# Weight preparation reordered: ScalarE's rounding one row later, three staging buffers, and the weights' stores and loads on another queue in the gated block

## The chip, the cores and the metric

The kernel runs on one core of a Trainium2 chip. The metric is the device time of one execution in microseconds (us). The parts of the core are TensorE (PE in the profile, its weight loads PEld), VectorE (DVE), ScalarE (ACT), GpSimd (POOL) and SyncE (SP). Each of them takes its instructions in the order in which they were issued. SyncE and GpSimd here mostly start transfers (DMAs); a transfer that has to wait for something holds up all that stands behind it in the same queue.

## The reference

Two blocks run one after the other. The first is attention with a hash: for each of 4 x 8 heads of 768 positions and 64 features, six sign bits of `q @ proj` and `k @ proj` give a bucket, and a query attends only to keys of its own bucket.

```python
scores = scale * np.matmul(q, k.transpose(0, 1, 3, 2))
scores = np.where(mask, scores, -1000000000.0)
attn = np.exp(scores - max); attn = attn / (sum + 1e-09)
out = np.matmul(attn, v)
```

The second is a gated block on the 3072 x 512 matrix that the heads make side by side:

```python
g = x @ w_gate                    # 512 x 1536
silu = g * (1.0 / (1.0 + np.exp(-g)))
val = x @ w_val
return (silu * val @ w_out)       # 1536 x 512
```

The three weight matrices come as 64-bit floats.

## The kernel before

**Attention part.** Heads are worked on in 16 pairs; the first four pairs are the first batch. A pair is two halves of 384 queries, and a half is what is called a row here: six units (`score(u)`, one per 128 keys). A unit is four score matmuls, two with `qT`/`kT` and two with the bits `qb`/`kb`, and two exponentials on ScalarE (L431). After the six units of a row come the 24 products with v (`attend`, L442). VectorE adds the exponentials of a row (`add`, L459 and L463), ScalarE copies the result out (L452), and a pair later the sums are made (`total`, L474, its copy L477), inverted (L483), spread by transfers over SyncE's queue, and the result is normalized (`norm`, L498). For the first batch the normalized result is split in three parts for the second block (`split`, L201, L204, L208); for the other batches it goes to memory (`kept_x`). Queries and keys are transposed on TensorE with copies on ScalarE (L342, L345) for the first pairs (`n <= NP`, 4) and on VectorE for the rest (L396).

**Weight preparation.** The weights are cut into 36 pieces of 128 x 512 doubles. Each piece is loaded into a word buffer (L116), and turned into three 32-bit parts in a staging buffer, and the staging buffer is stored (`ram`, L154) to be read again once per batch. This runs beside the attention, and what is left of it beside the first batch of the gated block. For piece i:

- `scale(i)`: two ScalarE passes (L123, L124), from the word buffer into the staging buffer and back into the word buffer.
- VectorE: shift (L141), sign (L143), addition (L146).
- ScalarE: the rounding (L147), which reads what L146 wrote.
- VectorE: the subtraction (L150) and the remainder (L152); then the store (L154).

`prepare()` is a generator with one VectorE step between two yields; `prepare_on(n)` runs n steps. Each row issues five steps (pairs 1 to 3) or four (the others) at its end, behind all else of the row, 134 of 180 in all; each atom of the gated block issues one. `scale_ahead()` is called between a row's scores and its products with v, and once after these; it issues the scaling of the next piece when at most two pieces are open. There are four word buffers and two staging buffers. All loads and stores of pieces but the first two loads stand on GpSimd's queue. The order of all this is the order of the calls; nothing plans it anew.

**Gated block.** For each of 4 batches, 12 blocks of columns (`U`: four groups of matmuls, tiles `a` and `n`, for gate and value; two atoms each) and 4 output steps (`D`: six chunks, tile `o`). All matmuls are at L584. PSUM holds four double banks in turn. The three parts of a weight piece are read into a ring of seven buffers (`bring`, L190), on GpSimd's queue, which also carries the pieces still in preparation. Three blocks before a batch ends, the next batch's `kept_x` is loaded on SyncE's queue (L700) into word buffers (`spare`) and split, one step per atom. The last pair's result and its spread sums sit in word buffers too; their inversion and normalization are issued at the 6th and the 14th atom of the block.

Of the kernel before, what the change touches and what calls it, by code (L numbers as in the profile page):

```python
# [19 lines left out]
def kernel(  # L20
# [20 lines left out]
    nc = tc.nc  # L41
    PSUM = bass.MemoryType.PSUM
    B, H, S, D = q.shape
    NBITS = proj.shape[1]
    P = 128
# [4 lines left out]
    NP = H // 2  # L50
# [4 lines left out]
    PIECE = 512  # L55
# [7 lines left out]
    STEP = 4096.0  # L63
    TOWARD = 1 - 2.0**-13

    konst = ctx.enter_context(tc.tile_pool(name="konst", bufs=1))
    wordp = ctx.enter_context(tc.tile_pool(name="wordp", bufs=4))
    stagep = ctx.enter_context(tc.tile_pool(name="stagep", bufs=2))
    small = ctx.enter_context(tc.tile_pool(name="small", bufs=2))
    even_x = ctx.enter_context(tc.tile_pool(name="even_x", bufs=1))  # L70
    ringp = ctx.enter_context(tc.tile_pool(name="ringp", bufs=7))
    dram = ctx.enter_context(tc.tile_pool(name="dram", bufs=1, space=bass.MemoryType.DRAM))
    ctx.enter_context(tc.manual_schedule())
# [3 lines left out]
    def r32(t):  # L77
        return t.bitcast(FP32R)
# [16 lines left out]
    n = 0  # L95
# [8 lines left out]
    NPIECE = len(pieces)  # L104
    ram = [dram.tile([P, 3, PIECE], FP32R, tag=f"ram{i}", name="ram") for i in range(NPIECE)]
    words = {}
    staged = {}
    progress = {"scaled": 0, "kept": 0}

    def load_words(count, queue=nc.gpsimd):  # L110
        for i in range(len(words), min(count, NPIECE)):
            words[i] = t = wordp.tile([P, PIECE, 2], I32, tag="words", name="words")
            to = t.rearrange("p f w -> p (f w)")
            if len(pieces[i].shape) == 3:
                to = to.rearrange("p (j c) -> p j c", j=NJ)
            queue.dma_start(to, pieces[i])  # L116

    def scale(i):
        t = words[i]
        staged[i] = st = stagep.tile([P, 3, PIECE], FP32, tag="stage", name="stage")  # L120
        top = t.rearrange("p f w -> p (f w)").bitcast(U16)
        top = top.rearrange("p (f w) -> p f w", w=4)[:, :, 1]
        nc.scalar.activation(st[:, 1], t[:, :, 1].bitcast(FP32), AF.Copy, scale=2.0**-112)  # L123
        nc.scalar.activation(t[:, :, 0], top, AF.Copy, scale=2.0**-13 * (1 + 2.0**-17))  # L124
        progress["scaled"] = i + 1

    def scale_ahead():
        i = progress["scaled"]
        if i < NPIECE and i < progress["kept"] + 2 and i in words:
            scale(i)  # L130

    def prepare():
        for i in range(NPIECE):
            load_words(i + 1)
            if i not in staged:
                scale(i)
            t, st = words[i], staged[i]
            lo, hi = t[:, :, 0], t[:, :, 1]
            w = st[:, 1]
            wi = w.bitcast(I32)  # L140
            nc.vector.tensor_single_scalar(wi, wi, 3, op=ALU.logical_shift_left)  # L141
            yield True
            nc.vector.scalar_tensor_tensor(out=wi, in0=hi, scalar=-(1 << 31), in1=wi,  # L143
                                           op0=ALU.bitwise_and, op1=ALU.bitwise_or)
            yield True
            nc.vector.tensor_tensor(wi, wi, lo, op=ALU.add)  # L146
            nc.scalar.activation(r32(st[:, 0]), w, AF.Copy, scale=TOWARD)  # L147
            load_words(i + 4)
            yield True
            nc.vector.tensor_tensor(r32(w), w, st[:, 0], op=ALU.subtract)  # L150
            yield True
            nc.vector.scalar_tensor_tensor(out=r32(st[:, 2]), in0=w, scalar=-STEP, in1=st[:, 0],  # L152
                                           op0=ALU.mult, op1=ALU.add)
            nc.gpsimd.dma_start(ram[i].bitcast(FP32), st)  # L154
            progress["kept"] = i + 1
            yield True

    preparing = prepare()

    def prepare_on(n):  # L160
        for _ in range(n):
            next(preparing, None)
# [33 lines left out]
    def split(x, b, pr, pool):  # L196
        xparts[b, pr] = t = pool.tile([P, 3, S], FP32R, tag=f"x{pr}", name="xparts")
        h, l, d = (t[:, i] for i in range(3))

        def high():  # L200
            nc.scalar.activation(h, x, AF.Copy, scale=TOWARD / STEP)  # L201

        def low():
            nc.vector.scalar_tensor_tensor(out=l, in0=h.bitcast(FP32), scalar=-STEP, in1=x,  # L204
                                           op0=ALU.mult, op1=ALU.add)

        def diff():
            nc.vector.tensor_tensor(d, h.bitcast(FP32), l.bitcast(FP32), op=ALU.subtract)  # L208

        return [high, low, diff]  # L210
# [3 lines left out]
    def attention(scope):  # L214
# [80 lines left out]
        for h in range(2):  # L295
# [6 lines left out]
                                op=ALU.mult)  # L302
# [18 lines left out]
        for i in range(RING):  # L321
            t = fixed.tile([P, 2, AW], FP32, tag=f"A{i}", name="A")
# [5 lines left out]
        load_words(2, nc.sync)  # L328
        for name, queue in (("q", nc.sync), ("k", nc.gpsimd), ("v", nc.sync)):
            fetch(1, name, queue)  # L330
        load_words(4)

        T = {}
        bits = {}
# [74 lines left out]
        acc = {}  # L409
        av = {}  # L410
        xT = {}
        mean = {}
        waiting = []

# [19 lines left out]
        def attend(u):  # L434
            n, half, c = units[u]
            a = weights(u)
            if c == 0:
                av[n] = av_ps.tile([P, 512], FP32, tag="av", name="av")
            ps = av[n]
            width = AW if half == 0 else HQ  # L440
            for h in range(2):
                nc.tensor.matmul(ps[h * D : (h + 1) * D, 0:width], raws["v", n][:, h, c, :],  # L442
                                 a[:, h, 0:width], start=c == 0, stop=c == NCH - 1)
            if c == NCH - 1:
                if half == 0:
                    if n == len(pairs) - 1:
                        xT[n] = spare()
                    else:
                        xT[n] = xp.tile([P, S], FP32, tag="xT", name="xT")
                    mean[n] = small.tile([P, 1], FP32, tag="e", name="e")  # L450
                    nc.scalar.activation(mean[n], ps[:, HQ : HQ + 1], AF.Copy, scale=EPS)
                nc.scalar.copy(xT[n][:, half * HQ : (half + 1) * HQ], ps[:, 0:HQ])  # L452
# [29 lines left out]
        def invert(n, few):  # L482
            nc.vector.reciprocal(few, few)  # L483
            s = sums[n % 2]
            nc.sync.dma_start(s, few)
            if n == len(pairs) - 1:
                t = spare().rearrange("p (x q) -> p x q", x=2)
            else:
                t = att.tile([P, 2, HQ], FP32, tag="r", name="r")
            flat = s.rearrange("p e -> (p e)").rearrange("(h x t) -> h (x t)", h=2, t=HQ)  # L490
            for h in range(2):
                nc.sync.dma_start(t[h * D : (h + 1) * D].rearrange("p x t -> p (x t)"),
                                  flat[h : h + 1].to_broadcast([D, 2 * HQ]))
            return lambda: norm(n, t)
# [13 lines left out]
        rest = []  # L508
# [48 lines left out]

    left = []

    def spare():  # L560
        t = wordp.tile([P, PIECE, 2], I32, tag="words", name="words")
        return t.rearrange("p f w -> p (f w)")[:, 0:S].bitcast(FP32)

    with ExitStack() as scope:
        attention(scope)

    def gated_block(scope):
        xs = [even_x, scope.enter_context(tc.tile_pool(name="odd_x", bufs=1))]  # L570
        hidp = scope.enter_context(tc.tile_pool(name="hidp", bufs=4))
        gatep = scope.enter_context(tc.tile_pool(name="gatep", bufs=2))
        outp = scope.enter_context(tc.tile_pool(name="outp", bufs=1))
# [41 lines left out]
        def atoms_of(kind, n):  # L615
# [33 lines left out]
            else:  # L649
# [35 lines left out]
                for c in range(NCH):  # L685
# [2 lines left out]
                        end(c)  # L688
                    yield chunk

        tails = []
        splits = []
        count = [0]
        for kind, n in order:
            if kind == "U":
                b, f = divmod(n, NF)
                if f == NF - NQ and b + 1 < B:
                    for pr in range(NP):
                        x = spare()
                        nc.sync.dma_start(x, kept_x[b + 1, pr])  # L700
                        splits += split(x, b + 1, pr, xs[(b + 1) % 2])
            if kind == "D" and n == B * NF // NQ - 1:
                finish(tails)
            for atom in atoms_of(kind, n):
                tail = atom()
                finish(tails)
                if tail:
                    tails.append(tail)
                if splits:
                    splits.pop(0)()  # L710
                count[0] += 1
                if left and count[0] in (6, 14):
                    left.append(left.pop(0)())
                    left[:] = [f for f in left if f]
                prepare_on(1)

    with ExitStack() as scope:
        gated_block(scope)
# [32 lines left out]
```

## Time and profile before

| | |
|---|---|
| median of 14 runs | 990.16 us (987.4 to 992.84) |
| the profiled execution | 992.84 us, its span 991.0 us |
| busy: TensorE, VectorE, ScalarE | 952.0, 674.8, 471.8 us |
| mean TensorE clock granted | 0.986 |
| first matmul of the gated block | at 385.47 us |

In a timeline row stand start and duration in us, the engine, the line of the kernel, the operation, the tiles as out<-in, the shapes, how many instructions were merged, and in brackets the idle time before it with what ended it. In a table of waits stand the total in us, how often, and the longest. In a table of stretches the numbers after the stretch are its length, the busy time of each engine with its count of instructions, the TensorE clock granted, the share of time the DMA engines were busy, and GB/s. In a row of grouped instructions the count is followed by the busy time, the mean duration of one in ns, and the engine's idle time before them with what ended it.

### The profile page before, as it was taken

Reading aid. Unit: us, or ns where it says so; the run is one execution under the profiler, and the core shown is the slowest. Engines: PE = TensorE matmul, PEld = TensorE weight load, DVE = VectorE, ACT = ScalarE, POOL = GpSimd, SP = SyncE. Lnnn points to the kernel's source line nnn. Section 1 sums busy time; section 2 is a strip of 40 time slices with the busy share of each in tenths; the row PEclk is TensorE's granted clock in tenths of the full one; section 3 lists DMA queues with packets and bytes.
Section 4 is the critical chain, followed back from the end, with each engine's and each line's share of the span. In section 5 each row is a group of like instructions: output and inputs, shape, how many; then the busy total and the mean of one; then the engine's idle time right before and its main releaser. Section 6 shows DMA issues by size and latency. Waiting matters only on the chain.

```text
span 991.0 us, 14470 instructions
## 1 busy us (share of the span) xinstructions
PE 952.0 (96%) x5413; PEld 726.8 (73%) x5413; DVE 674.8 (68%) x868; ACT 471.8 (48%) x882; POOL 125.1 (13%) x248
## 2 busy tenths in 40 slices
PE   8988899989899899999999999999999999999998
PEld 3444444444444346989999999999999999999996
DVE  4667678778878586868886546586546586546556
ACT  6867766877677485444322332322232322232221
POOL 3110010100101011131210110110110110110100
PEclk9989999999999899999999999999999999999999
DMA  6554566766878667499955854655854655654641
GB/s 181 175 154 133 160 173 139 212 181 188 202 170 217 198 242 251 165 353 374 344 201 187 321 191 157 224 190 191 319 189 161 223 186 193 259 186 165 223 160 64
DMA packets 134262, 203.22 MB, mean 205 GB/s; under 512 B 92912, under 2 KB 98512, under 8 KB 134192
## 3 DMA queue, kind: packets, MB, share of 16 engines
q0 software_dynamic: 31008, 159.79, 45.1%
q1 hardware_dynamic: 102384, 42.30, 17.3%
q8 instruction: 43, 0.70, 0.3%
q10 hardware_dynamic: 800, 0.20, 0.1%
q14 instruction: 27, 0.22, 0.1%
HBM read 162.01 MB, written 39.42 MB: 203 GB/s over the span
## 4 chain that ended last, share of the span: by engine, by line
PE 58%; DVE 1%; issue 1%; DMA 0%; ACT 0%; POOL 0%; POOLq 0%; DVEq 0%; ACTq 0%
PE a L584 27%; PE o L584 18%; PE n L584 13%; DVE o L676 0%; DVE o L673 0%; DMA ram<-stage 0%; ACT stage L123 0%; DVE words L498 0%; DVE hid L640 0%; DVE g L632 0%; DVE stage L143 0%; ACT words L124 0%; POOL words L116 0%; ACT o L671 0%; DVE stage L141 0%
## 5 line engine op out<-in xcount | busy, mean ns | idle before, releaser
L584 PE MATMUL a<-xparts,ring 128*128 128x384 f32 x1536 | 283.5, 335 | 1.9 <-ACT row L477 1.9
L584 PEld LDWEIGHTS a<-xparts,ring 128*128 128x128 f32 x1536 | 269.3, 188 | 3.8 <-ACT row L477 2.6
L584 PE MATMUL o<-ring,hid 128*128 128x512 f32 x864 | 199.4, 390 | 2.1 <-DVE o L676 2.1
L428 PE MATMUL sc<-qT,kT 64*128 64x384 f32 x768 | 176.4, 523 | 22.6 <-ACT A L431 22.6
L584 PEld LDWEIGHTS o<-ring,hid 128*128 128x128 f32 x864 | 161.8, 188 | 35.6 <-DVE o L676 2.5
L431 ACT ACTIVATE A<-sc 128x384 f32<-128x384 f32 x384 | 156.5, 503 | 9.1 <-PE sc L428 8.6
L584 PE MATMUL n<-xparts,ring 128*128 128x384 f32 x768 | 148.9, 335 | 0.0
L428 PEld LDWEIGHTS sc<-qT,kT 64*128 64x128 f32 x768 | 79.5, 193 | 93.7 <-issue 48.2
L463 DVE TENSOR_TENSOR acc<-acc,A 128x768 f32<-128x768 f32 x128 | 122.7, 958 | 25.0 <-ACT A L431 14.0
L584 PEld LDWEIGHTS n<-xparts,ring 128*128 128x128 f32 x768 | 135.0, 188 | 0.0
L442 PE MATMUL av<-A,vraw 128*64 128x386 f32 (+1 forms) x768 | 131.6, 491 | 0.0
L190 POOL DMA_DIRECT2D ring<-ram x144 | 76.2, 531 | 427.4 <-PE n L584 269.6
L632 DVE TENSOR_TENSOR v<-v,n 128x768 f32<-128x768 f32 x48 | 45.8, 954 | 104.6 <-PE n L584 103.1
L442 PEld LDWEIGHTS av<-A,vraw 128*64 128x64 f32 x768 | 52.4, 137 | 73.0 <-issue 62.0
L626 ACT ACTIVATE g<-a 128x768 f32<-128x768 f32 x48 | 38.9, 810 | 127.1 <-PE a L584 122.6
L637 ACT ACTIVATE hid<-v 128x768 fp32r<-128x768 f32 x48 | 40.7, 847 | 117.5 <-DVE v L636 117.5
L428 PE MATMUL sc<-qb,kb 64*128 64x384 bf16 x384 | 79.5, 335 | 5.2 <-DMA qb<-qb 4.6
L634 ACT ACTIVATE g<-g 128x768 f32<-128x768 f32 x48 | 40.6, 847 | 89.6 <-DVE g L632 89.6
L676 DVE TENSOR_TENSOR o<-o 128x512 f32<-128x512 f32 x96 | 66.0, 687 | 22.1 <-ACT o L671 19.7
L632 DVE TENSOR_TENSOR g<-g,n 128x768 f32<-128x768 f32 x48 | 45.6, 950 | 35.0 <-PE n L584 34.9
L154 POOL DMA_DIRECT2D ram<-stage x36 | 19.5, 542 | 369.1 <-issue 142.9
L640 DVE SCALAR_TENSOR_TENSOR hid<-hid,v 128x768 fp32r<-128x768 f32 x48 | 45.9, 956 | 26.2 <-ACT hid L637 26.2
(77 smaller groups left out, 712.4 us busy)
## 6 DMA issues: line engine op xcount, KB each, us to landing
ring<-ram POOLq DMA_DIRECT2D x144, 768.0 KB, 5.6
ram<-stage POOLq DMA_DIRECT2D x36, 768.0 KB, 5.0
vraw<-in_v_dram SPq DMA_DIRECT2D x16, 384.0 KB
words<-in_moe_w_out_dram POOLq DMA_DIRECT2D x12, 512.0 KB, 7.4
out_dram<-o SPq DMA_DIRECT2D x24, 256.0 KB
r<-sums SPq DMA_DIRECT2D x30, 192.0 KB
words<-in_moe_w_gate_dram POOLq DMA_DIRECT2D x11, 512.0 KB, 6.8
words<-in_moe_w_val_dram POOLq DMA_DIRECT2D x11, 512.0 KB, 7.5
```

What stands on the lines that cost most here:

```text
L190: nc.gpsimd.dma_start(t.bitcast(FP32), ram[at].bitcast(FP32))
L428: nc.tensor.matmul(sc[h], x["k", n][rows, ks], x["q", n][rows, qs], start=start, stop=not start)
L431: nc.scalar.activation(weights(u)[:, h, 0:HQ], sc[h], AF.Exp, scale=SCALE * (OFF / 2 if n <= NP else 1.0))
L442: nc.tensor.matmul(ps[h * D : (h + 1) * D, 0:width], raws["v", n][:, h, c, :], a[:, h, 0:width], start=c == 0, stop=c == NCH - 1)
L463: nc.vector.tensor_tensor(acc[n, half], acc[n, half], a[:, :, 0:HQ], op=ALU.add)
L584: nc.tensor.matmul(ps, w, x, start=start, stop=stop)
L626: nc.scalar.activation(two(z), ops[what][2], AF.Copy, scale=STEP + 1)
L632: nc.vector.tensor_tensor(two(z), two(z), n_, op=ALU.subtract)
L634: nc.scalar.activation(z, z, AF.Silu)
L637: nc.scalar.activation(h, val, AF.Copy, scale=TOWARD / STEP)
L640: nc.vector.scalar_tensor_tensor(out=l, in0=h.bitcast(FP32), scalar=-STEP, in1=val, op0=ALU.mult, op1=ALU.add)
L676: nc.vector.tensor_tensor(accs[c], accs[c], t[:, 1], op=ALU.subtract)
```

## The change

- Three word buffers instead of four, three staging buffers instead of two. Loads run up to piece i+2 instead of i+3. In the attention part scaling may run three pieces ahead of the stores (two in the gated block).
- The rounding of a piece is no longer issued with its addition. It goes on a list, `unrounded`, and the next call of `scale_ahead()` issues it before any scaling. The subtraction, the remainder and the store of piece i-1 come after the addition of piece i.
- In the gated block the preparation's loads and stores are on SyncE's queue, and `scale_ahead()` is called after each atom's step. Before the first reload of `kept_x` the preparation is run to its end.
- The last pair's result and its spread sums go into a buffer that later holds a part of a batch's x (`odd_x`), not into word buffers.

```diff
-    wordp = ctx.enter_context(tc.tile_pool(name="wordp", bufs=4))
-    stagep = ctx.enter_context(tc.tile_pool(name="stagep", bufs=2))
+    wordp = ctx.enter_context(tc.tile_pool(name="wordp", bufs=3))
+    stagep = ctx.enter_context(tc.tile_pool(name="stagep", bufs=3))
...
+    odd_x = {NP - 1: ctx.enter_context(tc.tile_pool(name="odd_x", bufs=1))}
...
-    progress = {"scaled": 0, "kept": 0}
+    progress = {"scaled": 0, "kept": 0, "ahead": 3}
+    queues = [nc.gpsimd]
...
+    unrounded = []
+
+    def round_up():
+        st = staged[unrounded.pop(0)]
+        nc.scalar.activation(r32(st[:, 0]), st[:, 1], AF.Copy, scale=TOWARD)
+
     def scale_ahead():
+        if unrounded:
+            round_up()
         i = progress["scaled"]
-        if i < NPIECE and i < progress["kept"] + 2 and i in words:
+        if i < NPIECE and i < progress["kept"] + progress["ahead"] and i in words:
             scale(i)

     def prepare():
-        for i in range(NPIECE):
...
+        for i in range(NPIECE + 1):
+            if i < NPIECE:
...
+                nc.vector.tensor_tensor(wi, wi, lo, op=ALU.add)
+                unrounded.append(i)
+                load_words(i + 3)
+                yield True
+            if i > 0:
+                while i - 1 in unrounded:
+                    round_up()
+                st = staged[i - 1]
+                w = st[:, 1]
+                nc.vector.tensor_tensor(r32(w), w, st[:, 0], op=ALU.subtract)
+                yield True
+                nc.vector.scalar_tensor_tensor(out=r32(st[:, 2]), in0=w, scalar=-STEP,
+                                               in1=st[:, 0], op0=ALU.mult, op1=ALU.add)
+                queues[0].dma_start(ram[i - 1].bitcast(FP32), st)
+                progress["kept"] = i
+                yield True
...
                     if n == len(pairs) - 1:
-                        xT[n] = spare()
+                        t = odd_x[NP - 1].tile([P, 3, S], FP32, tag=f"x{NP - 1}", name="lastx")
+                        xT[n], spread[n] = t[:, 0], t[:, 1]
...
-                t = spare().rearrange("p (x q) -> p x q", x=2)
+                t = spread[n].rearrange("p (x q) -> p x q", x=2)
...
+        queues[0] = nc.sync
+        progress["ahead"] = 2
...
                 if f == NF - NQ and b + 1 < B:
+                    while next(preparing, None):
+                        pass
                     for pr in range(NP):
...
                 prepare_on(1)
+                scale_ahead()
```

More of the change, by code (lines that the diff above doesn't have):

```diff
@@ L107, with load_words @@
     staged = {}
-    progress = {"scaled": 0, "kept": 0}
-    def load_words(count, queue=nc.gpsimd):
+    progress = {"scaled": 0, "kept": 0, "ahead": 3}
+    queues = [nc.gpsimd]
+    def load_words(count, queue=None):
+        queue = queue or queues[0]
         for i in range(len(words), min(count, NPIECE)):
@@ L125, in scale @@
         progress["scaled"] = i + 1
+    unrounded = []
+    def round_up():
+        st = staged[unrounded.pop(0)]
+        nc.scalar.activation(r32(st[:, 0]), st[:, 1], AF.Copy, scale=TOWARD)
     def scale_ahead():
+        if unrounded:
+            round_up()
         i = progress["scaled"]
-        if i < NPIECE and i < progress["kept"] + 2 and i in words:
+        if i < NPIECE and i < progress["kept"] + progress["ahead"] and i in words:
             scale(i)
     def prepare():
-        for i in range(NPIECE):
[L134 to L156, printed above, removed]
@@ new lines, in prepare @@
+        for i in range(NPIECE + 1):
+            if i < NPIECE:
+                load_words(i + 1)
+                if i not in staged:
+                    scale(i)
+                t, st = words[i], staged[i]
+                lo, hi = t[:, :, 0], t[:, :, 1]
+                wi = st[:, 1].bitcast(I32)
+                nc.vector.tensor_single_scalar(wi, wi, 3, op=ALU.logical_shift_left)
+                yield True
+                nc.vector.scalar_tensor_tensor(out=wi, in0=hi, scalar=-(1 << 31), in1=wi,
+                                               op0=ALU.bitwise_and, op1=ALU.bitwise_or)
+                yield True
[9 more added lines that the diff above has]
+                nc.vector.tensor_tensor(r32(w), w, st[:, 0], op=ALU.subtract)
+                yield True
+                nc.vector.scalar_tensor_tensor(out=r32(st[:, 2]), in0=w, scalar=-STEP,
+                                               in1=st[:, 0], op0=ALU.mult, op1=ALU.add)
+                queues[0].dma_start(ram[i - 1].bitcast(FP32), st)
+                progress["kept"] = i
+                yield True
@@ L330, in attention @@
             fetch(1, name, queue)
-        load_words(4)
+        load_words(3)
         T = {}
@@ L411, in attention @@
         xT = {}
+        spread = {}
         mean = {}
@@ L558 @@
     left = []
-    def spare():
-        t = wordp.tile([P, PIECE, 2], I32, tag="words", name="words")
-        return t.rearrange("p f w -> p (f w)")[:, 0:S].bitcast(FP32)
     with ExitStack() as scope:
@@ L569, in gated_block @@
     def gated_block(scope):
-        xs = [even_x, scope.enter_context(tc.tile_pool(name="odd_x", bufs=1))]
+        rest = scope.enter_context(tc.tile_pool(name="odd_x_rest", bufs=1))
+        xs = [dict.fromkeys(range(NP), even_x), {**dict.fromkeys(range(NP - 1), rest), **odd_x}]
         hidp = scope.enter_context(tc.tile_pool(name="hidp", bufs=4))
@@ L697, in gated_block @@
                 if f == NF - NQ and b + 1 < B:
+                    while next(preparing, None):
+                        pass
                     for pr in range(NP):
-                        x = spare()
+                        t = wordp.tile([P, PIECE, 2], I32, tag="words", name="words")
+                        x = t.rearrange("p f w -> p (f w)")[:, 0:S].bitcast(FP32)
                         nc.sync.dma_start(x, kept_x[b + 1, pr])
-                        splits += split(x, b + 1, pr, xs[(b + 1) % 2])
+                        splits += split(x, b + 1, pr, xs[(b + 1) % 2][pr])
             if kind == "D" and n == B * NF // NQ - 1:
```

## The prediction, made before the changed kernel ran

> **What bounds the kernel now.** I read the page first, then busy time by stretch, then who waits for whom on TensorE and ScalarE, then the timelines around the stalls.
>
> ```profile
> span 991.0 us, 14470 instructions
> PE 952.0 (96%) x5413; PEld 726.8 (73%) x5413; DVE 674.8 (68%) x868; ACT 471.8 (48%) x882; POOL 125.1 (13%) x248
> PEclk9989999999999899999999999999999999999999
> ```
>
> TensorE is busy for 96% of the span, so only its 39 us of idle time and the stretches at a lower clock can be won. The stretches below are cut at the row-sum matmuls (tile `sum`), one group per head pair: first pair 1 alone, then pairs 2 to 5, pairs 6 to 13, pair 14 alone, pair 15, and the gated block in two parts.
>
> ```profile
> core 0: us, PE busy (x) PEld busy (x) DVE busy (x) ACT busy (x) POOL busy (x), PEclk, DMA share, GB/s
> 33.17:54.90 21.73, 21.73 (x150) 10.12 (x149) 14.65 (x19) 19.44 (x43) 1.30 (x2) 1.00 0.63 188
> 54.90:161.12 106.22, 93.95 (x571) 45.26 (x569) 77.56 (x103) 75.39 (x168) 9.70 (x16) 0.92 0.57 157
> 161.12:344.70 183.58, 168.81 (x1090) 77.56 (x1088) 144.80 (x194) 126.88 (x293) 16.99 (x29) 0.98 0.73 188
> 344.70:365.38 20.68, 20.43 (x138) 8.89 (x136) 16.36 (x23) 17.08 (x40) 2.06 (x4) 1.00 0.73 254
> 365.38:385.47 20.09, 18.18 (x127) 8.04 (x125) 16.73 (x23) 14.72 (x35) 3.44 (x7) 1.00 0.66 234
> 435.33:991.00 555.67, 550.67 (x2922) 518.12 (x2921) 353.11 (x436) 172.51 (x225) 72.47 (x137) 1.00 0.60 217
> ```
>
> Two pairs run clean: pair 1 (which still transposes on TensorE) in 21.73, pair 14 in 20.68, both at full clock. Measured by these, pairs 2 to 5 lose 106.22 - 2 x 21.73 - 2 x 20.68 = 21.4 us, and pairs 6 to 13 lose 183.58 - 8 x 20.68 = 18.1 us. From 435.33 on TensorE idles only in the last 5 us (555.67 - 550.67): nothing to win there. The losses have names:
>
> ```profile
> PE sc L428 <- ACT A L431: 22.6, 10, 4.7
> PE sc L428 <- DMA qb<-qb: 4.6, 4, 1.6
> PE o L584 <- DVE o L676: 2.1, 1, 2.1
> PE a L584 <- ACT row L477: 1.9, 1, 1.9
> ```
>
> ```profile
> ACT stage L147 <- DVE stage L146: 57.6, 26, 8.4
> ACT stage L123 <- DMA ram<-stage: 9.8, 6, 3.2
> ```
>
> Ten times TensorE waits for an exponential (L431), and ScalarE itself stands 57.6 us before the rounding L147, whose input is VectorE's addition L146. One such place, ScalarE, then VectorE, then TensorE:
>
> ```profile
> 54.95 0.48 ACT L452 COPY xT<-av 128x384 f32<-128x384 f32 x1
> 59.03 0.63 ACT L147 ACTIVATE stage<-stage 128x512 fp32r<-128x512 f32 x1 [3.60 <-DVE stage L146]
> 59.57 1.62 ACT L431 ACTIVATE A<-sc 128x384 f32<-128x384 f32 x4
> ```
>
> ```profile
> 51.67 1.01 DVE L498 SCALAR_TENSOR_TENSOR xT<-xT,e,r 128x768 f32<-128x768 f32 x1
> 54.82 0.96 DVE L208 TENSOR_TENSOR xparts<-xparts 128x768 fp32r<-128x768 f32 x1
> 58.31 0.69 DVE L146 CUSTOM_DVE_ANT_0 stage<-words,stage 128x1024 uint16<-128x1024 uint16 x1
> ```
>
> ```profile
> 53.09 0.92 PE L428 MATMUL sc<-qT,kT 64*128 64x384 f32 x4
> 60.09 2.03 PE L428 MATMUL sc<-qT,kT 64*128 64x384 f32 x4 [3.33 <-ACT A L431]
> ```
>
> ScalarE is free at 55.43 and the next row's scores are already there, but the rounding is next in its queue, and VectorE reaches the addition at 58.31, after normalizing and splitting the pair before. TensorE fills its banks, stops 3.33 us, and afterwards four matmuls take 2.03 where 0.92 is usual.
>
> **The change part by part.** No instruction is added or removed: 36 pieces keep their two scalings, one rounding, five VectorE steps, one load and one store. What changes is order, buffers and queue.
>
> *The rounding a row later.* In the attention part the rounding of piece i comes after the next row's twelve exponentials. By then the addition is long done: here it ends at 59.00, and the exponentials of the row begun at 53.09 end at about 59.5: a pair of 20.43 with two times 4.11 of products with v (row below) leaves (20.43 - 8.22) / 2 = 6.1 us of scores per row, and one exponential is 1.62 / 4 = 0.4. So the 57.6 us wait goes, and with it what hangs on it: the 22.6 us of TensorE stalls, the slow stretches behind them, and most of the waits for `qb`, whose signs stand in the same ScalarE queue. Together that is the 21.4 + 18.1 = 39.5 us above. VectorE's own wait for the rounding goes too.
>
> *What comes due next.* The next thing ScalarE can stand on is L123, the scaling into a staging buffer that must have been stored. Three buffers do not loosen this, for the scaling also runs one piece further ahead and the store comes five steps later. VectorE's five steps and the store:
>
> ```profile
> L146 DVE CUSTOM_DVE_ANT_0 stage<-words,stage 128x1024 uint16<-128x1024 uint16 x36 | 24.7, 685 | 2.0 <-ACT g L634 0.5
> L152 DVE SCALAR_TENSOR_TENSOR stage<-stage 128x512 fp32r<-128x512 f32 x36 | 24.6, 684 | 0.8
> L141 DVE TENSOR_SCALAR stage<-stage 128x512 int32<-128x512 int32 x36 | 15.1, 419 | 10.7 <-ACT stage L123 10.7
> ram<-stage POOLq DMA_DIRECT2D x36, 768.0 KB, 5.0
> ```
>
> ```profile
> 38.30 0.88 ACT L345 ACTIVATE kT<-tps 128x384 f32<-128x384 f32 x2
> ```
>
> In a row with normalization and split, five steps (L143 and L150 like L146) take 4 x 0.685 + 0.419 = 3.2 us from 55.8 on, so the store goes out at 59.0 and lands at 64.0. ScalarE, through with exponentials at 59.5, with two copies of the next transposes (0.88) at 60.3 and with the rounding (0.63) at 60.9, waits 3.1 us. TensorE has its products with v (4.11, below) and some two score units in its banks meanwhile; I reckon 1.2 us of stall is left. There are four such rows, one for each pair of the first batch: between 0 and 4.8 us, taken 4. Rows without the split end VectorE's work 3 us earlier and should have no wait. For pairs 6 to 13 VectorE is busy 144.80 / 8 = 18.1 us per pair of 20.68: it keeps up, two or so us behind ScalarE, and the store lands about 1 us after ScalarE asks for it. Such waits exist already:
>
> ```profile
> 303.27 0.68 ACT L123 ACTIVATE stage<-words 128x512 f32<-128x512 f32 x1 [3.23 <-DMA ram<-stage]
> 348.92 4.11 PE L442 MATMUL av<-A,vraw 128*64 128x386 f32 x24
> 315.69 0.32 PE L428 MATMUL sc<-qb,kb 64*128 64x384 bf16 x1 [1.46 <-DMA qb<-qb]
> ```
>
> A wait of 3.23 stopped no score matmul, since 4.11 us of products with v cover it, but it left the signs late and 1.46 us of `qb` wait. So per pair 0 to 1.46; I take 0.4, nearer to nothing since the expected wait is a third of 3.23: 8 x 0.4 = 3.2 us (bounds 0 and 11.7). One place is of another kind:
>
> ```profile
> 330.13 0.23 DVE L483 RECIPROCAL few<-few 128x12 f32<-128x12 f32 x1 [4.63 <-DMA few<-row]
> 333.18 2.02 PE L428 MATMUL sc<-qT,kT 64*128 64x384 f32 x4 [4.71 <-ACT A L431]
> ```
>
> VectorE stands 4.63 us for a small transfer that left beside ring loads. The change does not touch that. The rounding no longer passes it on, but the store is then 4.63 late: a wait of some 5.6, of which 3.2 is covered; 2.4 stays (bounds 0 and 4.71).
>
> *Three word buffers.* Piece i+2 is now loaded where i+3 was, and scaled when two pieces are stored less: the load goes out one and a half rows (about 15.5 us) ahead of its scaling, against three and a half. It takes
>
> ```profile
> DMA to landing us min/median/max: 4.0/7.2/15.3
> ```
>
> so it costs nothing unless nearly all are at the maximum. Behind a late one stand the scaling and then the exponentials.
>
> *The transition and the gated block.* The last pair's result and spread sums get their own buffer and no longer hold word buffers.
>
> ```profile
> 385.47 4.34 PE L584 MATMUL a<-xparts,ring 128*128 128x384 f32 x16 [1.91 <-ACT row L477]
> 395.50 2.93 PE L584 MATMUL a<-xparts,ring 128*128 128x384 f32 x16
> 421.10 0.76 POOL L116 DMA_DIRECT2D words<-in_moe_w_gate_dram  x1 [16.29 <-DVE words L498]
> 430.50 0.66 ACT L123 ACTIVATE stage<-words 128x512 f32<-128x512 f32 x1 [4.66 <-issue]
> 432.99 2.34 PE L584 MATMUL o<-ring,hid 128*128 128x512 f32 x9 [2.13 <-DVE o L676]
> ```
>
> At 385.47 the row copy stood behind a rounding; without it 1.91 + (4.34 - 2.93) = 3.3 us can go, of which I leave 1 for a late store. At 432.99 the chain is a word load that sat 16.29 us on GpSimd for the last normalization, so a late scaling, so a late output copy. With loads and stores on SyncE's queue and no normalization in a word buffer, 2.1 us goes. Moved are ten pieces' stores and their loads. On SyncE they stand ahead of the last pair's sums and, later, of the four reloads per batch; each waits for a VectorE step that is next anyway, and the 24 output stores come after the weights are done. The fourth reload now waits for the first split, two atoms (some 4 us) of the ten it has. Inside the block the rounding still follows its addition at once, as now, behind 4 double banks.
>
> The page "DMA: Bandwidth & Descriptors" of the Trainium skill, section "Issuing engines are not separate DMA queues", says that starting transfers from another engine saves only the sequencer's issue time. Against it stands the 16.29 us row, where the queue waited for a buffer and not for issue time. By that rule the 2.1 us would stay.
>
> *Sum.* The profiled execution took 992.84 us, 1.84 around its 991.0 span. Removed 39.5 + 3.3 + 2.1 = 44.9; come back 4 + 3.2 + 2.4 + 1 = 10.6; net 34.3, which gives 958.5. This execution is the slowest of the 14 (median 990.16). TensorE's work is fixed, so the quicker ones have shorter stalls, and what is left of stalls should be shorter too: I put 957.5.
>
> **The rivals.**
>
> *A: the store takes the rounding's place.* The chain addition, remainder, store, landing, scaling is as long as the one removed. For it: L123 waits 9.8 us already, and rows get shorter while the landing's 5.0 does not. Against: those waits cost TensorE little. All bounds at their upper ends without the clock: 11.7 + 4.8 + 4.7 + 1.9 = 23.1 come back, 971.
>
> *B: the queue move does nothing.* The word loads still come late and the wait before the output matmul stays: 957.5 + 2.1 = 959.6. The 16.29 us row speaks against it. The rule of the Trainium skill's page above would have it so.
>
> *C: the wait is not removed.* VectorE is a whole row behind, so the rounding finds its addition undone again: about 990. Against: 18.1 busy of 20.68.
>
> *D: slower.* At the words' load: with three buffers a landing beyond 15.5 + 4.1 = 19.6 us stops TensorE at each of some 26 pieces (the attention part issues 134 of the 180 VectorE steps, five to a piece). It decides against the whole gain from 34.3 / 26 = 1.3 us more, that is landings of 21 us throughout; the time would then be above 993, say 998 at 21.2. The largest of all landings is 15.3.
>
> **How the numbers follow.** Forecast 0.62, A 0.24, B 0.06, C 0.04, D 0.04. The low end is everything removed and nothing back, 992.84 - 44.9 = 947.9, less 1 for a typical execution: 947. The high end holds A and a few us over it: 975. A measurement of this kernel tells about 0.2% from no change. Faster: forecast, A, B and half of C, 0.94; same 0.02; slower 0.04.
>
> **What would show it.** Right: no row of L147 waiting for L146 in the attention part, score matmuls waiting for L431 under 8 us in all, a full clock up to 385, pairs of 20.7 to 22.5, the first gated matmul near 350, no wait at the first output chunk. Of A: L123 waiting for `ram<-stage` for over 30 us, with score matmuls behind it. Of B: the output wait still there. Of D: L123 waiting for word loads. The prediction is wrong if pairs 6 to 13 stay above 22 us.

## The result and the profile after

The changed kernel takes 964.07 us (median of 10), against 990.22 us before (median of 48): a ratio of 0.9736, 95% interval 0.9718 to 0.9754. It is 26 us faster where 32.7 were forecast; 964.07 lies 6.6 us above the forecast of 957.5 and inside its range.

The page of the changed kernel (profiled execution 963.32 us):

```profile
span 961.5 us, 14459 instructions
PE 941.0 (98%) x5413; PEld 715.9 (74%) x5413; DVE 672.2 (70%) x868; ACT 473.7 (49%) x882; POOL 115.2 (12%) x231
```

What TensorE waits for, and then ScalarE's two waits around the weight pieces (the line numbers have moved: scores L446, exponentials L449, rounding L135, addition L158, first scaling L127):

```profile
PE hps L372 <- DVE qT L413: 7.6, 2, 7.1
PE sc L446 <- DMA qb<-qb: 4.4, 4, 2.7
PE sc L446 <- DVE kb L386: 1.5, 3, 0.8
PE a L600 <- ACT row L496: 0.6, 1, 0.6
PE sc L446 <- ACT A L449: 0.2, 1, 0.2
```

```profile
ACT stage L127 <- DMA ram<-stage: 16.3, 11, 3.1
ACT stage L135 <- DVE stage L158: 12.5, 4, 6.0
```

Score matmuls waited 22.6 us for exponentials before and wait 0.2 now. ScalarE's wait before the rounding fell from 57.6 us to 12.5, all four of them in the gated block. Its wait for the staging store rose from 9.8 to 16.3 us and stops no score matmul for more than that 0.2. But there is a wait of 7.1 us that was not there: the hash matmuls stand for VectorE's transposes.

The stretches, cut at the row sums as before: pair 1, pairs 2 to 4, 5 and 6, 7 to 11, 12 and 13, 14, and the gated block:

```profile
core 0: us, PE busy (x) PEld busy (x) DVE busy (x) ACT busy (x) POOL busy (x), PEclk, DMA share, GB/s
33.24:54.98 21.74, 21.74 (x151) 10.13 (x149) 15.20 (x20) 19.16 (x43) 2.60 (x4) 1.00 0.65 196
54.98:119.61 64.63, 64.63 (x434) 31.16 (x433) 56.07 (x74) 56.17 (x127) 5.83 (x10) 1.00 0.63 173
119.61:168.03 48.42, 44.69 (x275) 19.48 (x273) 39.25 (x54) 35.92 (x80) 5.17 (x8) 0.93 0.75 182
168.03:269.25 101.22, 100.91 (x682) 44.24 (x680) 88.35 (x119) 80.80 (x183) 9.65 (x16) 1.00 0.77 203
269.25:311.94 42.69, 40.73 (x274) 17.69 (x273) 35.08 (x48) 31.46 (x73) 4.92 (x8) 1.00 0.81 210
311.94:341.11 29.17, 22.05 (x138) 9.48 (x136) 18.86 (x27) 16.25 (x39) 2.10 (x4) 0.88 0.72 190
359.88:961.50 601.62, 596.79 (x3168) 561.64 (x3168) 385.87 (x482) 194.49 (x255) 73.54 (x139) 1.00 0.62 222
```

Profile against profile the span is 29.5 us shorter. Pairs 1 to 13, between the same row sums, take 311.94 - 33.24 = 278.7 us where they took 344.70 - 33.17 = 311.5: 32.8 less. Pair 14 takes 29.17 where it took 20.68: 8.5 more. Pair 15 with the transition takes 18.8 for 20.1, and the gated block 601.6 for 605.5. Pairs 7 to 11 now run at 20.2 each, with 0.3 us of idling in all five. Most of what is still lost sits in two places, pairs 5 and 6, and pair 14; pairs 12 and 13 lose another 2.2 us by the same measure.

The first place, TensorE and SyncE's queue:

```profile
143.42 0.47 PE L446 MATMUL sc<-qb,kb 64*128 64x384 bf16 x1 [2.69 <-DMA qb<-qb]
143.42 1.75 PE L446 MATMUL sc<-qT,kT 64*128 64x384 f32 x4
```

```profile
131.95 0.34 SPq L504 DMA_DIRECT2D sums<-few  x1
135.29 1.15 SPq L511 DMA_DIRECT2D r<-sums  x2
136.54 0.58 SPq L389 DMA_DIRECT2D qb<-qb  x1
137.17 5.54 SPq L271 DMA_DIRECT2D qraw<-in_q_dram  x4
```

The signs were ready at 133.95, but the queue stood at `r<-sums`, waiting for `sums<-few` to land, until 135.29. The bits left at 136.54 beside the reads of q and k and came almost 7 us later. After 2.69 us of idling the granted clock is 0.50, and four matmuls take 1.75 us instead of 0.92.

The second place, VectorE, TensorE, SyncE, and GpSimd's queue beside it:

```profile
328.12 0.98 DVE L413 STREAM_TRANSPOSE kT<-kraw 128x768 f32<-128x768 f32 x1 [8.69 <-DMA kraw<-in_k_dram]
```

```profile
330.01 0.85 PE L372 MATMUL hps<-qT,hash 128*32 128x384 f32 x2 [7.12 <-DVE qT L413]
```

```profile
305.81 7.14 SPq L271 DMA_DIRECT2D qraw<-in_q_dram  x4
312.99 10.46 SPq L271 DMA_DIRECT2D kraw<-in_k_dram  x4
```

```profile
314.84 0.54 POOL L171 DMA_DIRECT2D ram<-stage  x1 [8.10 <-ACT A L449]
315.37 0.53 POOL L207 DMA_DIRECT2D ring<-ram  x1
315.89 0.53 POOL L120 DMA_DIRECT2D words<-in_moe_w_out_dram  x1
316.42 0.53 POOL L207 DMA_DIRECT2D ring<-ram  x1
```

Starting the four reads of k took 10.46 us where it usually takes 2.77, and VectorE stood 8.69 us for them. A store, two ring loads and a word load were started on GpSimd's queue meanwhile. In the kernel before, the same four reads had all been started when the next such burst came, 1.3 us later:

```profile
339.48 2.77 SPq L254 DMA_DIRECT2D kraw<-in_k_dram  x4
343.57 0.54 POOL L154 DMA_DIRECT2D ram<-stage  x1 [22.68 <-ACT xT L452]
```

### The profile page after: what moved, and what is told of

Its sections match the earlier page's. It is cut to its first block, busy times and chain, and to the rows that moved or that the text cites. A ratio compares the mean times of both kernels' runs of the same rounds, so it can differ in the third digit from the quotient of the medians.

```text
span 961.5 us, 14459 instructions
## 1 busy us (share of the span) xinstructions
PE 941.0 (98%) x5413; PEld 715.9 (74%) x5413; DVE 672.2 (70%) x868; ACT 473.7 (49%) x882; POOL 115.2 (12%) x231
## 2 busy tenths in 40 slices
DMA packets 135798, 203.22 MB, mean 211 GB/s; under 512 B 92912, under 2 KB 100560, under 8 KB 135728
## 4 chain that ended last, share of the span: by engine, by line
PE 89%; DMA 4%; ACT 2%; SPq 2%; DVE 2%; issue 1%; ACTq 0%; DVEq 0%
PE a L600 28%; PE o L600 20%; PE n L600 14%; PE sc L446 14%; PE av L460 10%; DMA qb<-qb 2%; SPq L271 2%; ACT A L449 1%; PE hps L372 1%; PE sum L493 1%; PE tps L359 1%; DMA ram<-stage 1%; DMA qraw<-in_q_dram 1%; DMA xram<-xT 1%; ACT qb L377 1%
## 5 line engine op out<-in xcount | busy, mean ns | idle before, releaser
L449 ACT ACTIVATE A<-sc 128x384 f32<-128x384 f32 x384 | 157.7, 508 | 22.8 <-PE sc L446 22.3
L446 PE MATMUL sc<-qT,kT 64*128 64x384 f32 x768 | 167.1, 509 | 0.2 <-ACT A L449 0.2
L446 PEld LDWEIGHTS sc<-qT,kT 64*128 64x128 f32 x768 | 69.8, 190 | 71.4 <-issue 52.4
L446 PE MATMUL sc<-qb,kb 64*128 64x384 bf16 x384 | 69.3, 326 | 5.9 <-DMA qb<-qb 4.4
L689 DVE SCALAR_TENSOR_TENSOR o<-o 128x512 f32<-128x512 f32 x72 | 49.5, 687 | 12.0 <-PE o L600 11.4
```

The costliest lines, as they stand in the source:

```text
L446: nc.tensor.matmul(sc[h], x["k", n][rows, ks], x["q", n][rows, qs], start=start, stop=not start)
L449: nc.scalar.activation(weights(u)[:, h, 0:HQ], sc[h], AF.Exp, scale=SCALE * (OFF / 2 if n <= NP else 1.0))
L689: nc.vector.scalar_tensor_tensor(out=accs[c], in0=t[:, 0], scalar=STEP + 1, in1=accs[c], op0=ALU.mult, op1=ALU.add)
```

## The experiments

Three theories were tested. The main one: the rounding behind its addition was the stall, and deferring it is the gain. Its rival: the third staging buffer or the new order of VectorE's steps did it. For what is left: the transfers of SyncE's queue come late, either by their order in that queue or because the DMA engines are full.

**Rounding at once again.**

```diff
                 unrounded.append(i)
+                round_up()
```

> The changed kernel, but the rounding is issued at once behind its addition again; buffers, queues and the late subtraction stay. If the deferral is what removed the stalls: the ten stalls before exponentials and the slow clock come back in the attention part, about 20 of the 25.6 us by which the gated block began earlier (359.88 against 385.47), so 980 to 988, with ScalarE waiting for the addition over 40 us in all. If the third staging buffer or the other order of VectorE's steps did it: 962 to 967.

Measured: 987.2 us, ratio 0.9952 (0.9925 to 0.9979). Its waits:

```profile
PE sc L447 <- ACT A L450: 17.8, 11, 3.7
ACT stage L135 <- DVE stage L158: 59.2, 24, 6.0
```

Both waits are back with almost their old sizes. Undoing the deferral takes back about 21 of the 26 us (the ratios 0.9952 and 0.9736, of 990 us); the buffers and the order without it are worth 0.5%.

**Two staging buffers.**

```diff
-    stagep = ctx.enter_context(tc.tile_pool(name="stagep", bufs=3))
+    stagep = ctx.enter_context(tc.tile_pool(name="stagep", bufs=2))
...
-    progress = {"scaled": 0, "kept": 0, "ahead": 3}
+    progress = {"scaled": 0, "kept": 0, "ahead": 2}
```

> The changed kernel with two staging buffers again (and scaling two pieces ahead at most). If the third buffer is what lets the deferral pay: each scaling must wait for the store of the piece two before, which now goes out a whole piece later, so ScalarE and VectorE stand some 5 us per piece and the time is 975 to 1000. If the order alone does it: 962 to 968.

Measured: 1098.73 us, ratio 1.1082 (1.1029 to 1.1135), worse than either theory had it.

```profile
ACT stage L127 <- DMA ram<-stage: 151.7, 27, 12.3
DVE stage L153 <- ACT stage L127: 129.4, 22, 8.5
PE sc L446 <- ACT A L449: 72.5, 14, 7.2
```

Here is rival A in full: ScalarE stands for the store, 5.6 us on average before each of 27 scalings, and takes TensorE with it. So the deferral needs the third buffer: without it the kernel is slower than before, and the other changes without the deferral are worth 0.5%.

**The gated block: which half of the edit removed its stall.**

```diff
-        queues[0] = nc.sync
```

> The changed kernel, but in the gated block the pieces' stores and loads stay on GpSimd's queue. If the queue move removed the 2.13 us stall at the first output step: that stall is back, about 966. If it was the last pair's buffers (no normalization in a word buffer any more): no stall there, 962 to 966, the same within the interval.

Measured: 967.11 us, ratio 0.9749 (0.9700 to 0.9797), above both times expected, but not to be told from the changed kernel. In its profile no output matmul waits, and TensorE has no gap where the stall was:

```profile
363.14:413.00 49.86, 49.86 (x271) 47.71 (x271) 39.12 (x56) 25.67 (x38) 12.78 (x22) 1.00 0.81 296
```

The other half undone, the last pair's result and sums in word buffers again:

```diff
-                        t = odd_x[NP - 1].tile([P, 3, S], FP32, tag=f"x{NP - 1}", name="lastx")
-                        xT[n], spread[n] = t[:, 0], t[:, 1]
+                        xT[n] = spare()
...
-                t = spread[n].rearrange("p (x q) -> p x q", x=2)
+                t = spare().rearrange("p (x q) -> p x q", x=2)
...
```

> The changed kernel, but the last pair's result and its spread sums sit in word buffers again; the queue move stays. If the last pair's own buffer removed the 2.13 us wait at the first output step: an output matmul waits for the output copy again for 1 to 3 us, or SyncE's queue stands behind the normalization. If the queue move alone is enough: no wait there.

Measured: 966.88 us in one execution, which says nothing about 2 us, but in its profile the wait is back:

```profile
406.77 2.33 PE L603 MATMUL o<-ring,hid 128*128 128x512 f32 x9 [1.91 <-DVE o L695]
```

That looks as if the buffer had removed the stall, and not the queue move. But the wait also stands in two profiles that keep both halves of the edit: 1.53 us in the kernel with VectorE's copies (below), and 1.97 us in the one that rounds at once, whose rows follow:

```profile
418.11 0.66 ACT L127 ACTIVATE stage<-words 128x512 f32<-128x512 f32 x1 [2.95 <-DMA ram<-stage]
428.49 2.33 PE L601 MATMUL o<-ring,hid 128*128 128x512 f32 x9 [1.97 <-DVE o L693]
```

In all three profiles the scaling ahead of the output step stood for a staging store (3.62 us here, 2.95 with the rounding at once, 2.45 with VectorE's copies); in the changed kernel the same scaling, at 392.29, stood for nothing. So the stall comes with a late scaling. With one profile of each half it isn't shown that either half of the edit removed it.

**The query bits from ScalarE's queue.**

```diff
-                nc.sync.dma_start(bits["q", n][high], bits["q", n][low])
+                nc.scalar.dma_start(bits["q", n][high], bits["q", n][low])
```

> The changed kernel, but the transfer that spreads the query bits (qb) is started from ScalarE's queue, right behind the signs it reads, and not from SyncE's queue behind the transfers of the sums. If the new 2.69 us wait at 143.42 and the slow clock behind it come from SyncE's queue: score matmuls wait for qb under 1.5 us in all and pairs 5 and 6 take about 20.5 each where they took 25.8 and 22.6, so 956 to 960. If the transfer itself is late because the DMA engines are full: the wait stays, 962 to 967. If starting a transfer costs ScalarE more than it gains: above 967.

Measured: 967.6 us, ratio 0.9751 (0.9701 to 0.9801): no gain that can be told.

```profile
PE hps L372 <- DVE qT L413: 9.1, 3, 8.0
PE sc L446 <- DMA qb<-qb: 5.9, 7, 1.9
```

The wait at 143 is gone, but seven smaller ones for `qb` add up to more than the four before. The order in the queue was only part of it: the transfer itself takes about 7 us beside the reads of q and k (started at 159.44, waited for until 166.90).

**Ring loads earlier, one in every second row.**

```diff
-            if u >= N - 7 * NCH:
+            if u >= N - 15 * NCH and half == 1 and len(held) < 7:
                 bring()
```

> The changed kernel, but the seven ring loads of the attention part are started one in every second row from the fifteenth row before its end on, and not one in each of its last seven rows. If the ring loads crowd out the reload of q and k, whose lateness is the 7.12 us wait at 330.01: that wait goes, with the slow clock behind it, pair 14 takes 20 to 22 where it took 29.2, so 954 to 958. If q and k are late for another reason (SyncE's queue, the faster rows): the wait stays somewhere in pairs 11 to 14, 962 to 967.

Measured: 968.87 us, ratio 0.9769 (0.9721 to 0.9817): a miss for both theories as I had priced them.

```profile
PE sc L446 <- DMA qb<-qb: 8.6, 6, 2.2
PE hps L372 <- DVE qT L413: 5.0, 3, 2.3
```

The 7.12 us wait is gone, as the first theory said, but its time came back in many small waits, most of them from pair 9 on, as the second said. That the ring loads crowd out the small transfers isn't shown by this run: two of the waits for `qb` that grew end at 166.99 (1.72 us, 0.18 in the changed kernel) and 210.06 (0.92 us), and the first ring load is started at 212.27.

**q and k in long rows.** The same bytes from the same queue in rows of 768 bytes instead of 128.

```diff
-                for x in range(D // BLOCK):
-                    at = h * D + x * BLOCK
+                for x in range(2):
+                    at = (2 * h + x) * (S // 4)
...
-                        blocks[at : at + BLOCK],
-                        src[b, 2 * pr + h][:, x * BLOCK : (x + 1) * BLOCK].rearrange(
-                            "(a p c) d -> p c a d", c=NCH, p=BLOCK))
+                        flat[:, at : at + S // 4],
+                        src[b, 2 * pr + h].rearrange("(p c) d -> p (c d)", c=NCH)[
+                            :, x * (S // 4) : (x + 1) * (S // 4)])
```

> The changed kernel, but from the sixth pair on q and k are read in rows of 768 bytes instead of 128, by as many transfers of the same size from the same queue; the 32 x 32 blocks then hold other elements, so the attention of these pairs is left out in the sense that it is computed on wrongly placed features, with the same instructions. If the new waits (kraw, few, sums, qb: the transfers of SyncE's queue) come from the DMA engines being full of small packets beside stores, words and ring loads: these waits go nearly all, pairs 5 to 14 take 20.1 to 20.6 each, 948 to 953. If they come from SyncE's order alone (each transfer behind the one before it): nothing changes, 962 to 968.

Measured: 957.53 us, ratio 0.9653 (0.9611 to 0.9696). DMA packets fell from 135798 to 79478. The page's line on them, pairs 7 to 12 in one stretch (columns as above), and TensorE's waits:

```profile
DMA packets 79478, 203.22 MB, mean 213 GB/s; under 512 B 25328, under 2 KB 44240, under 8 KB 79408
```

```profile
167.78:288.60 120.82, 120.82 (x818) 53.09 (x817) 105.85 (x143) 96.77 (x220) 10.92 (x18) 1.00 0.65 200
```

```profile
PE sc L445 <- DMA qb<-qb: 5.9, 2, 3.1
PE hps L371 <- DVE qT L412: 0.5, 1, 0.5
```

With fewer packets no read of k is late and these six pairs take 20.14 each. So the late k comes from the many small packets. Whether they fill the DMA engines or hold the queue that starts them isn't separated: one read of k was started in 0.43 us (median) instead of 0.66, and in 0.96 at most instead of 4.60. The two waits for `qb` that stay (2.80 and 3.10 us) are those in which the bits stand behind a late `r<-sums`, and pair 5 takes 25.90 us, as in the changed kernel (25.81). So each of the two explanations fits one of the two places, and my expectation, which offered them as alternatives, missed by some 5 us.

**q and k earlier.** A second buffer for raw q and k, and their loads in the first row of a pair.

```diff
-                                         bufs=1)
+                                         bufs=2)
...
-                if half == 1 and c == 2:
+                if half == 0 and c == 2:
                     load(n + 2, "qk")
```

> The changed kernel with a second buffer for raw q and k, and their loads for pair n+2 issued half a pair earlier, in the first row of pair n and not in its second. If the waits come from the moment at which the burst of q and k stands beside the query bits and before VectorE's transposes: the 7 us wait for kraw goes and the waits for qb shrink under 2 us, pair 14 near 20.5, pairs 5 and 6 near 21, so 950 to 956. If the DMA engines are full over the whole second half: the waits move to few and sums, 960 to 967.

Measured: 987.51 us, ratio 0.9951 (0.9926 to 0.9976); neither expectation held.

```profile
320.00 9.09 SPq L271 DMA_DIRECT2D qraw<-in_q_dram  x4
329.13 4.07 SPq L271 DMA_DIRECT2D kraw<-in_k_dram  x4
340.94 1.13 SPq L511 DMA_DIRECT2D r<-sums  x2
342.16 0.58 SPq L389 DMA_DIRECT2D qb<-qb  x1
```

```profile
PE sc L446 <- DMA qb<-qb: 27.1, 9, 8.2
```

k is never late now, but the eight reads, which took 13 us to start in the place shown, stand ahead of the sums and the bits. Score matmuls wait 27.1 us for the bits, 22.7 more than in the changed kernel, and the kernel is 23 us slower. How much of it is the order in the queue, and how much that the sums then take longer to land (7.6 us from 333.30 to the start of `r<-sums`), isn't separated.

**The query bits without a transfer.** By two VectorE copies, and by one copy on GpSimd:

```diff
-                nc.sync.dma_start(bits["q", n][high], bits["q", n][low])
+                for half in range(2):
+                    cols = slice(half * HQ, (half + 1) * HQ)
+                    nc.vector.tensor_copy(bits["q", n][high, cols], bits["q", n][low, cols])
...
+                nc.gpsimd.tensor_copy(bits["q", n][high], bits["q", n][low])
```

> The changed kernel, but the query bits are spread by two VectorE copies (0.25 us each where such copies stand now) and not by a transfer. If the wait for qb is a transfer of some 7 us started too late, behind the sums in SyncE's queue and beside the reads of q and k: no score matmul waits for qb, pairs 5 and 6 take 20.1 to 21.5, and q and k start some 2 us earlier, so 954 to 960. If VectorE, at 17.3 to 20.9 us busy per pair of 20.1, has no room for it: score matmuls wait for kb instead, 962 to 970.

> The same with one copy on GpSimd, which is idle but for starting transfers. If its queue is free at that moment: as with VectorE's copies or 1 to 3 us better, 953 to 959. If the copy stands behind a store that waits for VectorE: score matmuls wait for qb several us in each pair, above 970.

Measured: 963.38 us with VectorE, ratio 0.9708 (0.9665 to 0.9750), and 959.67 us with GpSimd, ratio 0.9679 (0.9642 to 0.9716). The interval of the second lies just below the changed kernel's. Its waits:

```profile
PE hps L372 <- DVE qT L413: 7.2, 1, 7.2
PE sc L446 <- DVE kb L386: 3.1, 6, 1.0
```

No wait for `qb` is left, and pairs 2 to 13 are almost free of stalls; pair 14 is as it was. On VectorE the copies cost about what they save: score matmuls then wait 5.3 us for `kb`.

**Ring loads elsewhere.** First VectorE's copies with the spread ring loads, then GpSimd's copy with the ring loads in the last four rows, after the last reads of q and k:

```diff
-            if u >= N - 7 * NCH:
-                bring()
+            if u >= N - 4 * NCH:
+                bring(1 if u == N - 4 * NCH else 2)
```

> VectorE's copies and the ring loads spread over fifteen rows, both. If the waits of pairs 5 and 6 and of pair 14 are two separate things: both gone, 948 to 955. If what is left of transfers still fills the DMA engines and the lateness only moves: 954 to 962.

> GpSimd's copy of the query bits, and the seven ring loads in the last four rows (1, 2, 2, 2), behind the last reads of q and k, and not in the last seven. If ring loads beside the reads of q and k make kraw late (7.2 us of wait before the hash matmuls of pair 14 and a slow clock behind it): that wait falls under 2 us, pair 14 takes 20.1 to 21.5, the first gated matmul is at 344 to 347, so 949 to 953. If kraw is late without them: 957 to 962. If the ring then fills too late for the gated block: its first blocks wait, above 962.

Measured: 967.2 us, ratio 0.9750 (0.9713 to 0.9787), for the first: the lateness only moves, and further than expected. The second takes 958.95 us (953.76 to 961.45), ratio 0.9686 (0.9659 to 0.9712). In its profiled execution, the quickest of the six (953.76), the hash matmuls wait for nothing and the first gated matmul is at 349.67:

```profile
PE sc L446 <- DVE kb L386: 4.9, 6, 2.0
PE a L600 <- ACT row L496: 1.5, 1, 1.5
```

So the 7 us wait needs the ring loads beside the reads of q and k: it is gone where they are moved (here and with the spread ring loads) and also where the reads have fewer packets. But the time is not what the first theory gave for it, and the median isn't below that of GpSimd's copy alone (0.9686 and 0.9679). What the slower of the six executions lose wasn't profiled and stays open. Both have intervals below the changed kernel's (0.9718 to 0.9754), though they were not run side by side with it.

## Why the prediction was right, point by point

- **The sum** came close in part by luck. Profile against profile 34.3 us were forecast and 29.5 measured. Pairs 1 to 13 gave 32.8 where 39.5 - 4 - 3.2 - 2.4 = 29.9 were forecast, pair 14 took 8.5 where nothing was, and the last pair, the transition and the gated block together gave 5.2 where 2.3 + 2.1 = 4.4 were. A removal missed in part, returns that hardly came and a loss that no term held offset each other. The rest of the 6.6 us is the 1 us that I took off for a typical execution, and the 0.75 us by which the profiled execution after lies below its median.
- **What bounds and why** held. The wait named (ScalarE, VectorE, TensorE) is the gain: undone alone it takes back about 21 us. Of the signs, score matmuls wait 0.2 us for exponentials and the rounding waits nowhere in the attention part, as I had said; but the clock is not full in pairs 5, 6 and 14, and the first gated matmul is at 359.88, not near 350.
- **The removal, 39.5 us** was too small and too large at once. Its baseline, 20.68 per clean pair, was not clean: pairs 7 to 11 take 101.22 / 5 = 20.24. But "most of the waits for `qb`" did not go: 4.6 us before, 4.4 after, now with a slow clock behind the longest. Pairs 5 and 6 lose 48.42 - 2 x 20.24 = 7.9 us. This step failed: I had put those waits down to late signs on ScalarE alone, and overlooked that the bits stand in SyncE's queue behind the sums, for which the queue stood until 135.29.
- **The store coming due, 4 + 3.2 us** was mis-sized. ScalarE does stand for it (16.3 us, 11 times, the longest 3.1), as described, but score matmuls lose 0.2 us to it, so almost nothing of the 7.2 came.
- **The one odd place, 2.4 us** (bounds 0 and 4.71) failed. VectorE's longest wait for such a small transfer is now 2.7 us instead of 4.63, and score matmuls don't feel it. But I also said that the change does not touch the burst of ring loads. It does: the burst, which had followed the reads of k by 1.3 us, now met them, and pair 14 went from 20.68 to 29.17, 8.5 us, outside my bounds.
- **Three word buffers at no cost** held: ScalarE waits for no word load. **The transition, 2.3 us net**: 0.60 of stall is left of 1.91, and the first sixteen matmuls take 3.04 instead of 4.34, so 2.6 us went.
- **The gated block, 2.1 us** came in the changed kernel's profile, but neither of its two named causes is shown: the wait stands again in two profiles that keep both. The rule of the Trainium skill ("DMA: Bandwidth & Descriptors", "Issuing engines are not separate DMA queues") agrees with the queue move, which changes nothing that can be told (967.11 without it, 964.07 with it, the intervals overlapping). The 16.29 us row, which I had held against the rule, shows a queue standing for a buffer, and of that the rule says nothing.
- **The rivals.** A is real but shows only with two staging buffers (1098.73). B has the queue move right, as far as one profile shows, but the wait before the output matmul went. C and D did not come. Both real losses, the bits and the reads of k, are transfers that come late on SyncE's queue, and no rival had that mechanism.

## What to carry to other kernels

An engine that works in order should not be given an operation until its input is sure to be there; issuing it one loop body later cost nothing here but one more buffer, and without that buffer it was worse than not doing it at all. When a stall is removed, look again at every small transfer that had its time hidden by the stall: its place in its queue, what that queue waits for, and what large transfers start in the same microsecond. A short copy on an idle engine can replace a small transfer that is slow to land: here GpSimd's copy, 0.8 to 1.5 us by the profile's rough spans, replaced one of 48 KB that took some 7 us.

## What the runs showed of the hardware

Starting a transfer is not of fixed length: in the changed kernel four reads of k, 96 KB each in 128-byte packets, were started in 2.77 us nine times out of eleven, in 4.08 us once, and in 10.46 us beside a store, a word load and two ring loads, and all that stood behind them in the queue waited. With two staging buffers the profiled execution spans 109 us more than the kernel before; TensorE idles 115 us instead of 39, and it is busy 33 us longer with the same matmuls, at a mean granted clock of 0.94 instead of 0.986.

TensorE ran slowly after less idling than I would have looked for: after 2.69 us at 143.42 in the changed kernel, while 1.19 us at 289.82 left the clock at 1.00. The Trainium skill ("TensorE: Matmul & The Clock Gate", "Part 1: The HAM clock gate (the "warmup" mystery)") says that the clock halves after at least one idle window of about 3.4 us. In the kernel before, an idle time of 1.91 us, up to 385.47, was enough, so the measurement differs from the page. There the clock was still 1.00 up to 386.90, 1.4 us after TensorE had restarted, then 0.50, and 1.00 again from 390.60. What sets the moment was not tried.
